# Attention with a double linear product: the weights' 64-bit words split on VectorE alone, with GpSimd left out

## The chip, the cores and the metric

The kernel runs on one core of one Trainium2 chip. The metric is the device time in microseconds, from three runs of the kernel before: 810.65 us median (810.63 to 811.8). One further execution was profiled, and the rows below come from it. PE is TensorE, PEld its loading of weights, DVE is VectorE, ACT is ScalarE, POOL is GpSimd, SP the engine that issues most loads.

## What is computed

Attention with a window and sinks (4 batches, 8 heads, 768 positions, 64 per head), then for all 3072 tokens a product of two linear projections, projected back. The text calls the second part the MoE, as the kernel does. The weights come as 64-bit floats, which the kernel reads as pairs of 32-bit words.

```python
scores = scale * np.matmul(q, k.transpose(0, 1, 3, 2))
keep = is_sink | in_window                 # pos < 4, or 0 <= rel < 128
a = softmax(where(keep, scores, -1e9))
x = (a @ v) as rows of 512                 # 3072 x 512
a = x @ w_a                                # 512 x 1536
b = x @ w_b
out = (a * b @ w_out)                      # 1536 x 512
```

## The kernel before

The tokens are taken in eight chunks of 2 to 4 tiles of 128 rows (CHUNKS). For each chunk the attention makes xf (four tiles of 128 features), `split_x` cuts it into a high half xh that TensorE reads in one pass (L667, ScalarE) and the rest xl (L668, VectorE), and `moe` runs 12 steps j over 128 of the 1536 inner features each: 12 matmuls for a, 12 for b (L686: high by high, high by low, low by high), their product g (L705 ScalarE, L711 VectorE), its halves gh (L714 ScalarE) and gl (L716), and one step later 3 matmuls per tile into the output (`project`, L695).

The attention of the first chunk runs alone: per unit (a head and a tile of rows) scores (L548, TensorE), the masked minimum (L555, VectorE), the exponential (L557, ScalarE), the normalisation (L559, L560, L562, VectorE), a transposition (L585) and the product with v (L602). Small copies for the sinks (L569) run on GpSimd. The attention of chunk c + 1 is woven into the MoE of chunk c, a few units per step, by `between`. The second chunk's attention has the same lines, with the normalisation on ScalarE (L564). From the third chunk on the attention is another form, in which GpSimd cuts q, k and v into halves (L345, L348).

There are 36 weight tiles of 128 x 512: a, b and o for each j, in this order. Each is loaded on SP's queue (L290) as 1024 32-bit words, low and high word in turns, and goes through stages that `weights_to` calls, one new tile per call:

- `weight_bits`: VectorE shifts the high word (L301) and joins sign and top bit to it (L303); ScalarE scales the low word (L302); GpSimd adds both (L305);
- three calls later `weight_high` (D1): ScalarE's cast to the high half (L312), into the tile that held the raw words;
- one call after that `weight_low` (D2): the low half (L317), a subtraction, on GpSimd for every third tile (all of b), else on VectorE.

The first seven calls lie in the first attention (from its step 18 on, every third step), the others in the first MoE, one in front of a's matmuls, one in front of b's and one in front of the projection of each j. Loads run up to 9 tiles ahead of the stage. gl (L716) runs on GpSimd for j below 10 and on VectorE for the last two.

Instructions given to `pin` (`keep_in_program_order`) keep the order of the program among themselves on their engine. All others, matmuls among them, are put where the framework's planner reckons that their operands are ready. L303, L305, L555, gl and the products g are such.

Of the kernel before, what the change touches and what calls it, by code (L numbers as in the profile page):

```python
# [7 lines left out]
F32 = mybir.dt.float32  # L8
# [5 lines left out]
ALU = mybir.AluOpType  # L14
# [3 lines left out]
B, H, S, D = 4, 8, 768, 64  # L18
DM, FF = 512, 1536
P = 128  # L20
# [3 lines left out]
NJ = FF // P  # L24
# [6 lines left out]
NEG = 8.0e9  # L31
BIG = 3.0e38
NIO = 6
POOL_LOW = (1, 3)
STEP0, STEPS = 18, 3
AHEAD, LOADS = 3, 9
D1, D2 = 3, 4
WARM = 8
H_MIN = 1.375 * 2.0 ** -12
H_SUM = 65536.0  # L40
# [1 line left out]
I_TOP2 = -1073741824  # L42
# [176 lines left out]
class Fast:  # L219
# [70 lines left out]
        self.nc.sync.dma_start(raw, self.src(kind)[j].bitcast(I32))  # L290
        self.raw[kind, j] = raw

    def low_engine(self, kind, j):
        return self.nc.gpsimd if (3 * j + "abo".index(kind)) % POOL_LOW[1] == POOL_LOW[0] else self.nc.vector

    def weight_bits(self, kind, j):
        nc, pin = self.nc, self.tc.keep_in_program_order
        rv = self.raw[kind, j].rearrange("p (n c) -> p n c", c=2)
        lo, hi = rv[:, :, 0], rv[:, :, 1]
        f = self.io([P, DM], I32, f"wf_{kind}{j}")  # L300
        pin(nc.vector.tensor_scalar(f, hi, 3, 0x3FFFFFF8, op0=ALU.logical_shift_left, op1=ALU.bitwise_and))  # L301
        pin(nc.scalar.activation(lo, lo.bitcast(U32), AF.Copy, scale=2.0 ** -29))  # L302
        nc.vector.scalar_tensor_tensor(out=f, in0=hi, scalar=I_TOP2, in1=f,  # L303
                                       op0=ALU.bitwise_and, op1=ALU.bitwise_or)
        nc.gpsimd.tensor_tensor(f, f, lo, op=ALU.add)  # L305
        del self.raw[kind, j]
        self.wf[kind, j] = f.bitcast(F32)

    def weight_high(self, kind, j):
# [3 lines left out]

    def weight_low(self, kind, j):
        wh, wl = self.wt[kind, j]
        e = self.low_engine(kind, j)
        i = e.tensor_tensor(wl, self.wf.pop((kind, j)), wh.bitcast(F32), op=ALU.subtract)  # L317
        if e is self.nc.vector:
            self.tc.keep_in_program_order(i)

    def check_weight(self, kind, j):

# [346 lines left out]
            xs.append((xh, xl))  # L669
        return xs  # L670

    def moe(self, row, nt, xf, between, weights_ahead, last):
        nc = self.nc
        n = nt * P
        tag = f"{row}"
        xs = self.split_x(xf, nt, tag)
        outs = [self.ps.tile([P, DM], F32, tag=("o0", "o1", "o2", "av")[i], name=f"o{tag}_{i}") for i in range(nt)]

        def half(kind, j):
            wh, wl = self.wt[kind, j]  # L680
            ps = self.ps.tile([P, 4 * P], F32, tag=kind, name=f"{kind}{tag}_{j}")
            for kk in range(NK):
                ksl = slice(kk * P, (kk + 1) * P)
                xh, xl = xs[kk]
                for i, (w, x) in enumerate(((wh, xh), (wh, xl), (wl, xh))):
                    nc.tensor.matmul(ps[:, :n], lhsT=w[:, ksl], rhs=x[:, :n],  # L686
                                     start=kk == 0 and i == 0, stop=kk == NK - 1 and i == 2)
            return ps

        def project(j, gh, gl):  # L690
            wh, wl = self.wt["o", j]
            for i in range(nt):
                sl = slice(i * P, (i + 1) * P)
                for k, (g, w) in enumerate(((gh, wh), (gh, wl), (gl, wh))):
                    nc.tensor.matmul(outs[i], lhsT=g[:, sl], rhs=w,  # L695
                                     start=j == 0 and k == 0, stop=j == NJ - 1 and k == 2)

        prev = None
        for j in range(NJ):
            if last and j == 2:  # L700
                self.ok = self.verdict(self.ps.tile([1, P], F32, tag="s", name="gp"))
            weights_ahead(3 * j)
            pa = half("a", j)
            g = self.mo.tile([P, max(n, 3 * P)], F32, tag="g", name=f"g{tag}_{j}", bufs=1)
            nc.scalar.copy(g[:, :n], pa[:, :n])  # L705
            between(3 * j)
            if last and j == NJ - 1:
                self.tc.mark_branch_hint_location("general", hint="LikelyTaken", engines=mybir.ALL_ENGINES)
            weights_ahead(3 * j + 1)
            pb = half("b", j)  # L710
            nc.vector.tensor_tensor(g[:, :n], pb[:, :n], g[:, :n], op=ALU.mult)  # L711
            gh = self.mo.tile([P, max(n, 3 * P)], F32R, tag="gh", name=f"gh{tag}_{j}")
            gl = self.mo.tile([P, max(n, 3 * P)], F32R, tag="gl", name=f"gl{tag}_{j}")
            nc.scalar.copy(gh[:, :n], g[:, :n])  # L714
            e = nc.vector if j >= NJ - 2 else nc.gpsimd
            e.tensor_tensor(gl[:, :n], g[:, :n], gh[:, :n].bitcast(F32), op=ALU.subtract)  # L716
            between(3 * j + 1)
            weights_ahead(3 * j + 2)
            if prev is not None:
                project(*prev)  # L720
            between(3 * j + 2)
            prev = (j, gh, gl)
        project(*prev)
        for i in range(nt):
            r = row + i * P
            o = self.mo.tile([P, DM], F32, tag=("gh", "gl")[i % 2], name=f"os{tag}_{i}")
            (nc.vector.tensor_copy if last and i == 1 else nc.scalar.copy)(o, outs[i])
            (nc.sync if last else nc.scalar).dma_start(self.out[r:r + P, :], o)
# [4 lines left out]
    def run(self, scalars, verdict):  # L733
        chunks = CHUNKS
        order = [(k, j) for j in range(NJ) for k in "abo"]
        done, loaded = [0], [0]

        def weights_to(n, ahead):
            while loaded[0] < min(n + ahead, len(order)):
                self.load_weight(*order[loaded[0]])  # L740
                loaded[0] += 1
            while done[0] < min(n + D2, len(order) + D2):
                k = done[0]
                for d, stage in ((D2, self.weight_low), (D1, self.weight_high), (0, self.weight_bits)):
                    if 0 <= k - d < len(order):
                        stage(*order[k - d])
                done[0] += 1

        b, t0, nt = chunks[0]

        pairs = [self.wp.tile([P, 2, nt * P], F32, tag=f"w_{k}{NJ - 1}", name=f"xf0_{k}") for k in "bo"]
        xf = [x[:, i, :] for x in pairs for i in range(2)]
        first = self.attention(b, t0, nt, xf, exact=True, alone=True)
        next(first)
        val = scalars()
        self.masks(val)
        self.verdict = lambda gp: verdict(val, gp)
        for k, _ in enumerate(first, 1):
            if k >= STEP0 and (k - STEP0) % STEPS == 0:
                weights_to(done[0] + 1 - D2, 4 + D2)  # L760
        for c, (b, t0, nt) in enumerate(chunks):
            gen = None
            if c + 1 < len(chunks):
                nb, nt0, nnt = chunks[c + 1]
                nxf = self.new_xf(c + 1)
                gen = self.attention(nb, nt0, nnt, nxf, exact=c == 0)
                steps = H * nnt + (6 if c else 5)
            taken = [0]

            def between(s):  # L770
                if gen is None:
                    return
                want = min(steps, -(-steps * (s + 1) // (3 * NJ - 3)))
                while taken[0] < want:
                    next(gen, None)
                    taken[0] += 1

            def ahead(s):
                j = s // 3
                weights_to(max(s + AHEAD, done[0] + 1 - D2), LOADS)  # L780
                if s % 3:
                    return
                k = (c - 2) * 8 + j - 2
                if c >= 2 and 2 <= j < 10 and k < len(order):
                    self.check_weight(*order[k])
                elif self.unchecked:
                    self.check_weight(None, 0)

            self.moe(b * S + t0 * P, nt, xf, between, ahead, c + 1 == len(chunks))
            if gen is not None:  # L790
                for _ in gen:
                    pass
                xf = nxf
        return val, self.ok
# [73 lines left out]
```

## Time and profile before

| | |
|---|---|
| median of three runs | 810.65 us |
| the profiled execution | 809.97 us |
| its span, first to last instruction | 808.1 us |
| TensorE busy | 787.8 us (97%) |
| VectorE, ScalarE, GpSimd busy | 433.8, 477.1, 381.0 us |
| additions L305 on GpSimd | 36, from 30 to 168 us |
| subtractions L317 | 12 on GpSimd, 24 on VectorE |
| gl L716 of the first MoE | 10 on GpSimd, 2 on VectorE |
| attention alone, first MoE | 0 to about 57.6 us, 57.6 to 188.5 us |

A matmul's end is modelled in such a profile, so a busy TensorE is not TensorE at its peak. A wait names the instruction that released the waiting one last. [...]

### The profile page before, as it was taken

Reading aid. Unit: us, or ns where it says so; the run is one execution under the profiler, and the core shown is the slowest. Engines: PE = TensorE matmul, PEld = TensorE weight load, DVE = VectorE, ACT = ScalarE, POOL = GpSimd, SP = SyncE. Lnnn points to the kernel's source line nnn. Section 1 sums busy time; section 2 is a strip of 40 time slices with the busy share of each in tenths; the row PEclk is TensorE's granted clock in tenths of the full one; section 3 lists DMA queues with packets and bytes.
Section 4 is the critical chain, followed back from the end, with each engine's and each line's share of the span. In section 5 each row is a group of like instructions: output and inputs, shape, how many; then the busy total and the mean of one; then the engine's idle time right before and its main releaser. Section 6 shows DMA issues by size and latency. Waiting matters only on the chain.

```text
span 808.1 us, 13597 instructions
## 1 busy us (share of the span) xinstructions
PE 787.8 (97%) x4457; PEld 697.4 (86%) x4457; DVE 433.8 (54%) x1427; ACT 477.1 (59%) x1384; POOL 381.0 (47%) x483
## 2 busy tenths in 40 slices
PE   8997999999999999999999999999999999999997
PEld 5655777778989999999999999999999999999996
DVE  6889877834663555445654455535554456430101
ACT  5775665636774766567774677647674678631111
POOL 1248665673772564626653466515646266301110
PEclk9999999999999999999999999999999999999999
DMA  8866430031221133413323133231334132001001
GB/s 311 299 219 256 172 103 21 11 95 63 67 67 63 46 108 115 119 59 103 102 89 102 65 107 105 93 105 48 108 115 124 54 105 61 1 2 39 1 1 41
DMA packets 44778, 76.11 MB, mean 94 GB/s; under 512 B 4640, under 2 KB 24224, under 8 KB 44704
## 3 DMA queue, kind: packets, MB, share of 16 engines
q1 hardware_dynamic: 41648, 69.70, 26.9%
q10 hardware_dynamic: 3024, 5.51, 1.8%
q8 instruction: 36, 0.59, 0.3%
q14 instruction: 38, 0.31, 0.1%
q0 software_dynamic: 32, 0.00, 0.0%
HBM read 68.90 MB, written 6.29 MB: 93 GB/s over the span
## 4 chain that ended last, share of the span: by engine, by line
PE 87%; DVE 8%; ACT 2%; issue 1%; POOL 0%; DVEq 0%; ACTq 0%; POOLq 0%
PE o L695 23%; PE a L686 23%; PE b L686 23%; PE t L451 4%; PE s L419 4%; PE av L467 3%; PE s L548 2%; PE av L602 1%; PE t L585 1%; PE t L602 1%; DVE wf_a L303 1%; DVE wf_a L301 1%; DVE p L562 1%; DVE g L711 1%; PE sk L492 1%
## 5 line engine op out<-in xcount | busy, mean ns | idle before, releaser
L686 PE MATMUL a<-xh,w_a 128*128 128x384 f32 (+2 forms) x768 | 218.9, 345 | 0.0
L686 PE MATMUL b<-xh,w_b 128*128 128x384 f32 (+2 forms) x768 | 215.2, 343 | 0.0
L695 PE MATMUL o<-w_o,gh 128*128 128x512 f32 x576 | 186.8, 404 | 0.0
L716 POOL TENSOR_TENSOR gl<-g,gh 128x384 fp32r<-128x384 f32 (+2 forms) x80 | 83.2, 1040 | 197.9 <-ACT gh L714 195.0
L686 PEld LDWEIGHTS a<-xh,w_a 128*128 128x128 f32 x768 | 138.7, 188 | 6.5 <-issue 1.5
L686 PEld LDWEIGHTS b<-xh,w_b 128*128 128x128 f32 x768 | 138.8, 188 | 4.5 <-issue 0.8
L711 DVE TENSOR_TENSOR g<-b,g 128x384 f32<-128x384 f32 (+2 forms) x96 | 53.4, 556 | 150.6 <-PE b L686 142.8
L686 PE MATMUL a<-xl,w_a 128*128 128x384 f32 (+2 forms) x384 | 129.2, 337 | 0.9 <-DVE xl L668 0.9
L686 PE MATMUL b<-xl,w_b 128*128 128x384 f32 (+2 forms) x384 | 129.0, 336 | 0.0
L695 PEld LDWEIGHTS o<-w_o,gh 128*128 128x128 f32 x576 | 104.0, 188 | 19.5 <-issue 1.0
L695 PE MATMUL o<-w_o,gl 128*128 128x512 f32 x288 | 113.7, 396 | 0.6 <-POOL gl L716 0.6
L714 ACT CAST gh<-g 128x384 fp32r<-128x384 f32 (+2 forms) x96 | 49.4, 514 | 79.7 <-DVE g L711 77.7
L705 ACT COPY g<-a 128x384 f32<-128x384 f32 (+2 forms) x96 | 45.1, 470 | 79.5 <-PE a L686 69.9
L430 ACT ACTIVATE p<-p,st 128x128 f32<-128x128 f32 (+1 forms) x144 | 71.4, 496 | 26.3 <-DVE st L429 25.4
L426 ACT ACTIVATE p<-p,st 128x128 f32<-128x128 f32 (+1 forms) x144 | 71.6, 497 | 8.4 <-DVE st L424 8.3
L686 PEld LDWEIGHTS a<-xl,w_a 128*128 128x128 f32 x384 | 72.4, 189 | 3.5 <-DVE xl L668 1.3
L686 PEld LDWEIGHTS b<-xl,w_b 128*128 128x128 f32 x384 | 72.4, 188 | 2.0 <-issue 0.3
L454 ACT CAST pt<-t 128x128 fp32r<-128x128 f32 (+1 forms) x144 | 50.4, 350 | 39.1 <-PE t L451 37.3
L455 DVE TENSOR_TENSOR pt<-t,pt 128x128 fp32r<-128x128 f32 (+1 forms) x144 | 57.1, 397 | 20.9 <-ACT pt L454 19.4
L695 PEld LDWEIGHTS o<-w_o,gl 128*128 128x128 f32 x288 | 54.1, 188 | 14.2 <-POOL gl L716 1.0
L345 POOL TENSOR_SCALAR qh<-qr 128x384 fp32r<-128x384 f32 x48 | 24.6, 512 | 75.3 <-PE s L419 43.8
L424 DVE CUSTOM_DVE_ANT_0 p<-s,mg 128x264 f32<-128x264 f32 x96 | 41.1, 428 | 34.7 <-PE s L419 34.4
(141 smaller groups left out, 1334.7 us busy)
## 6 DMA issues: line engine op xcount, KB each, us to landing
qr<-in_qT_dram SPq DMA_DIRECT2D x48, 192.0 KB, 2.6
raw_a<-in_wa_dram SPq DMA_DIRECT2D x12, 512.0 KB, 6.4
raw_b<-in_wb_dram SPq DMA_DIRECT2D x12, 512.0 KB, 5.7
raw_o<-in_wo_dram SPq DMA_DIRECT2D x12, 512.0 KB, 6.2
chk_a<-in_wa_dram SPq DMA_DIRECT2D x24, 256.0 KB, 2.7
chk_b<-in_wb_dram SPq DMA_DIRECT2D x24, 256.0 KB, 2.7
chk_o<-in_wo_dram SPq DMA_DIRECT2D x24, 256.0 KB, 2.7
out_dram<-os ACTq DMA_DIRECT2D x21, 256.0 KB, 2.1
```

The source lines that it names most:

```text
L419: nc.tensor.matmul(ps[:, :w], lhsT=q[:, i * P:(i + 1) * P], rhs=ks[:, c0:c0 + w], start=m == 0, stop=m == 1)
L424: nc.vector.tensor_tensor_reduce(out=p[:, :w], in0=ps[:, :w], in1=m, scale=-0.125, scalar=BIG, op0=ALU.add, op1=ALU.min, accum_out=st[:, 0:1])
L426: nc.scalar.activation(p[:, :w], p[:, :w], AF.Exp, bias=st[:, 0:1], scale=-1.0, accum_out=st[:, 1:2])
L430: nc.scalar.mul(p[:, :w], p[:, :w], st[:, 3:4])
L454: nc.scalar.copy(hs, tp[:, :n, :])
L455: nc.vector.tensor_tensor(ls, tp[:, :n, :], hs.bitcast(F32), op=ALU.subtract)
L686: nc.tensor.matmul(ps[:, :n], lhsT=w[:, ksl], rhs=x[:, :n], start=kk == 0 and i == 0, stop=kk == NK - 1 and i == 2)
L695: nc.tensor.matmul(outs[i], lhsT=g[:, sl], rhs=w, start=j == 0 and k == 0, stop=j == NJ - 1 and k == 2)
L705: nc.scalar.copy(g[:, :n], pa[:, :n])
L711: nc.vector.tensor_tensor(g[:, :n], pb[:, :n], g[:, :n], op=ALU.mult)
L714: nc.scalar.copy(gh[:, :n], g[:, :n])
L716: e.tensor_tensor(gl[:, :n], g[:, :n], gh[:, :n].bitcast(F32), op=ALU.subtract)
```

## The change

The addition L305 moves from `weight_bits` into a stage of its own, `weight_sum`, one call later, and from GpSimd to VectorE, pinned. L303 is pinned too. `weight_high` comes two calls after the bits instead of three, `weight_low` three instead of four. Every low half is taken on VectorE. `moe` learns by `weights_split` whether the weights are split already: in the first chunk they aren't, and gl is on VectorE for all twelve j; in the other chunks it stays where it was. Because D2 is one less, the count of loads issued in the first MoE is one ahead of before.

```diff
--- before.py
+++ after.py
@@ -31,10 +31,9 @@
 NEG = 8.0e9
 BIG = 3.0e38
 NIO = 6
-POOL_LOW = (1, 3)
 STEP0, STEPS = 18, 3
 AHEAD, LOADS = 3, 9
-D1, D2 = 3, 4
+D0, D1, D2 = 1, 2, 3
 WARM = 8
 H_MIN = 1.375 * 2.0 ** -12
 H_SUM = 65536.0
@@ -290,9 +289,6 @@
         self.nc.sync.dma_start(raw, self.src(kind)[j].bitcast(I32))
         self.raw[kind, j] = raw
 
-    def low_engine(self, kind, j):
-        return self.nc.gpsimd if (3 * j + "abo".index(kind)) % POOL_LOW[1] == POOL_LOW[0] else self.nc.vector
-
     def weight_bits(self, kind, j):
         nc, pin = self.nc, self.tc.keep_in_program_order
         rv = self.raw[kind, j].rearrange("p (n c) -> p n c", c=2)
@@ -300,10 +296,15 @@
         f = self.io([P, DM], I32, f"wf_{kind}{j}")
         pin(nc.vector.tensor_scalar(f, hi, 3, 0x3FFFFFF8, op0=ALU.logical_shift_left, op1=ALU.bitwise_and))
         pin(nc.scalar.activation(lo, lo.bitcast(U32), AF.Copy, scale=2.0 ** -29))
-        nc.vector.scalar_tensor_tensor(out=f, in0=hi, scalar=I_TOP2, in1=f,
-                                       op0=ALU.bitwise_and, op1=ALU.bitwise_or)
-        nc.gpsimd.tensor_tensor(f, f, lo, op=ALU.add)
-        del self.raw[kind, j]
+        pin(nc.vector.scalar_tensor_tensor(out=f, in0=hi, scalar=I_TOP2, in1=f,
+                                           op0=ALU.bitwise_and, op1=ALU.bitwise_or))
+        self.wf[kind, j] = f
+
+    def weight_sum(self, kind, j):
+
+        f = self.wf[kind, j]
+        lo = self.raw.pop((kind, j)).rearrange("p (n c) -> p n c", c=2)[:, :, 0]
+        self.tc.keep_in_program_order(self.nc.vector.tensor_tensor(f, f, lo, op=ALU.add))
         self.wf[kind, j] = f.bitcast(F32)
 
     def weight_high(self, kind, j):
@@ -313,10 +314,8 @@
 
     def weight_low(self, kind, j):
         wh, wl = self.wt[kind, j]
-        e = self.low_engine(kind, j)
-        i = e.tensor_tensor(wl, self.wf.pop((kind, j)), wh.bitcast(F32), op=ALU.subtract)
-        if e is self.nc.vector:
-            self.tc.keep_in_program_order(i)
+        self.tc.keep_in_program_order(
+            self.nc.vector.tensor_tensor(wl, self.wf.pop((kind, j)), wh.bitcast(F32), op=ALU.subtract))
 
     def check_weight(self, kind, j):
 
@@ -669,7 +668,7 @@
             xs.append((xh, xl))
         return xs
 
-    def moe(self, row, nt, xf, between, weights_ahead, last):
+    def moe(self, row, nt, xf, between, weights_ahead, last, weights_split):
         nc = self.nc
         n = nt * P
         tag = f"{row}"
@@ -712,7 +711,7 @@
             gh = self.mo.tile([P, max(n, 3 * P)], F32R, tag="gh", name=f"gh{tag}_{j}")
             gl = self.mo.tile([P, max(n, 3 * P)], F32R, tag="gl", name=f"gl{tag}_{j}")
             nc.scalar.copy(gh[:, :n], g[:, :n])
-            e = nc.vector if j >= NJ - 2 else nc.gpsimd
+            e = nc.gpsimd if weights_split and j < NJ - 2 else nc.vector
             e.tensor_tensor(gl[:, :n], g[:, :n], gh[:, :n].bitcast(F32), op=ALU.subtract)
             between(3 * j + 1)
             weights_ahead(3 * j + 2)
@@ -741,7 +740,7 @@
                 loaded[0] += 1
             while done[0] < min(n + D2, len(order) + D2):
                 k = done[0]
-                for d, stage in ((D2, self.weight_low), (D1, self.weight_high), (0, self.weight_bits)):
+                for d, stage in ((D2, self.weight_low), (D1, self.weight_high), (D0, self.weight_sum), (0, self.weight_bits)):
                     if 0 <= k - d < len(order):
                         stage(*order[k - d])
                 done[0] += 1
@@ -786,7 +785,7 @@
                 elif self.unchecked:
                     self.check_weight(None, 0)
 
-            self.moe(b * S + t0 * P, nt, xf, between, ahead, c + 1 == len(chunks))
+            self.moe(b * S + t0 * P, nt, xf, between, ahead, c + 1 == len(chunks), c > 0)
             if gen is not None:
                 for _ in gen:
                     pass
```

## Rows read from the trace of the kernel before

**Rows 1.** Stretches: us, busy PE, PEld, DVE, ACT, POOL (instructions), clock, DMA share, GB/s

```profile
20.00:57.60 37.60, 35.70 (x194) 22.65 (x193) 31.56 (x131) 29.38 (x87) 11.89 (x20) 1.00 0.73 254
57.60:88.00 30.40, 23.64 (x98) 17.56 (x98) 28.60 (x40) 18.33 (x40) 24.87 (x20) 0.94 0.65 245
...
100.00:146.00 46.00, 44.68 (x210) 33.71 (x209) 35.71 (x71) 29.06 (x65) 28.22 (x28) 1.00 0.19 60
...
188.50:802.00 613.50, 610.92 (x3625) 569.96 (x3624) 290.09 (x1057) 361.89 (x1100) 277.43 (x368) 1.00 0.24 73
```

**Rows 2.** Who TensorE waited for: us in all, times, longest us

```profile
PE s L548 <- DVE st L555: 5.9, 3, 5.3
...
PE a L686 <- DVE xl L668: 0.9, 1, 0.9
...
PE o L695 <- POOL gl L716: 0.6, 1, 0.6
```

**Rows 3.** Timeline, 75.5 to 82 us: start us, us, engine, line, operation, [idle before]

```profile
75.67 1.46 POOL L716 TENSOR_TENSOR gl<-g,gh 128x512 fp32r<-128x512 f32 x1
...
76.04 1.65 DVE L303 SCALAR_TENSOR_TENSOR wf_a<-raw_a,wf_a 128x512 int32<-128x512 int32 x1
...
78.21 1.48 DVE L301 TENSOR_SCALAR wf_b<-raw_b 128x512 int32<-128x512 int32 x1
...
79.73 1.65 DVE L303 SCALAR_TENSOR_TENSOR wf_b<-raw_b,wf_b 128x512 int32<-128x512 int32 x1
81.30 0.42 DVE L555 CUSTOM_DVE_ANT_0 p<-s,mg 128x264 f32<-128x264 f32 x1
...
81.78 0.81 PE L548 MATMUL s<-kx,qx 128*128 128x264 f32 x1 [5.25 <-DVE st L555]
```

**Rows 4.** The stretch behind the stall, columns as in rows 1

```profile
81.40:84.90 3.50, 3.12 (x11) 2.11 (x11) 2.61 (x9) 2.65 (x6) 2.07 (x3) 0.51 0.76 308
```

**Rows 5.** Single lines: engine, operation, count: shortest/median/longest ns, first to last start us

```profile
L301 DVE TENSOR_SCALAR wf_b<-raw_b x12: 396/415/1539, 32.3 to 157.6; 128x512 int32<-128x512 int32 x12
...
L303 DVE SCALAR_TENSOR_TENSOR wf_b<-raw_b,wf_b x12: 677/691/1677, 33.0 to 158.1; 128x512 int32<-128x512 int32 x12
...
L305 POOL TENSOR_TENSOR wf_b<-wf_b,raw_b x12: 1286/1306/1767, 33.8 to 161.2; 128x512 int32<-128x512 int32 x12
...
L317 DVE TENSOR_TENSOR w_a<-wf_a,w_a x12: 669/682/1783, 47.8 to 169.3; 128x512 fp32r<-128x512 f32 x12
...
L562 DVE TENSOR_SCALAR p<-p,st x21: 273/350/1237, 20.2 to 50.1; 128x264 f32<-128x264 f32 x16, 128x128 f32<-128x128 f32 x5
...
L668 DVE TENSOR_TENSOR xl<-xf_o,xh x2: 681/1252/1824, 46.3 to 57.5; 128x512 fp32r<-128x512 f32 x2
```

**Rows 6.** Busy time of L301 alone: 57.6 to 88, and 20 to 188.5

```profile
57.60:88.00 30.40, 8.08 (x9) 0.94 0.65 245
...
sum 168.50, DVE 29.66; mean DVE 9.89
```

**Rows 7.** The same of L303 alone

```profile
57.60:88.00 30.40, 9.03 (x9) 0.94 0.65 245
...
sum 168.50, DVE 33.18; mean DVE 11.06
```

**Rows 8.** The same of L317 alone, GpSimd's part second

```profile
57.60:88.00 30.40, 7.37 (x6) 5.18 (x3) 0.94 0.65 245
...
sum 168.50, DVE 24.05 POOL 17.95; mean DVE 8.02 POOL 5.98
```

**Rows 9.** The same of L562 alone, 20 to 57.6 us

```profile
20.00:57.60 37.60, 10.76 (x21) 1.00 0.73 254
```

**Rows 10.** Timeline: first matmul of j = 3; fifth a's low half, its first use

```profile
88.02 0.40 PE L686 MATMUL a<-xh,w_a 128*128 128x512 f32 x1
...
88.39 0.68 DVE L317 TENSOR_TENSOR w_a<-wf_a,w_a 128x512 fp32r<-128x512 f32 x1
...
98.56 0.50 PE L686 MATMUL a<-xh,w_a 128*128 128x512 f32 x1
```

## The prediction

> **What bounds the kernel now.** I read the busy time by stretches first [rows 1], because a mean over 808 us hides where TensorE stands still. From 188.5 us on, TensorE is busy 610.92 of 613.5 us; VectorE and GpSimd there cost nothing, and the change alters nothing in that part. The weights are split before that. 20 to 57.6 us is the second half of the first attention, which runs alone; at 57.6 us the first MoE gets its last inputs, and by 88 us it runs evenly. In 57.6 to 88 TensorE is busy 23.64 of 30.4 us at a mean granted clock of 0.94, while VectorE is busy 28.60. In 100 to 146 TensorE misses 1.3 us. So whatever the change can give, it must give almost wholly in that one stretch of 30 us.
>
> The table of who waited for whom names the 6.8 us lost there [rows 2]: one wait of 5.3 us of the scores (L548) for the softmax's first VectorE step (L555), 0.9 us for the low half of the attention output (L668), 0.6 us for gl on GpSimd (L716). In order of time [rows 3] the long one is plain: VectorE has L555 behind four weight instructions, and three of these take 1.48 to 1.65 us. GpSimd runs weight and gate subtractions beside them. [...]
>
> Why are they long? Each line has two durations [rows 5]: L301 takes 0.40 to 0.42 us or 1.5, L303 0.68 or 1.68, L317 0.67 or 1.78, the same form each time. The long durations lie beside a GpSimd instruction of this size [rows 3], the quiet ones beside none. GpSimd's own add also stretches, 1.29 to 1.77. I read it as one engine standing still while the other holds what both need.
>
> **The change, part by part.** *The queue.* Per weight VectorE gets one addition (L305) and, for every b, the subtraction (L317) that GpSimd had; per j of the first MoE the gate's subtraction, ten times. No row shows the integer addition on VectorE. Its nearest row is L303: the same 512 columns, int32, one input at a stride of two words, two inputs from SBUF: 0.68 to 0.69 us quiet. The ends are L301's 0.41 and L305's 1.29 on GpSimd [rows 5]; I take 0.69. Nothing here excludes that it is a little cheaper. Added: 36 x 0.69 + 12 x 0.675 + 10 x 0.675 = 39.7 us.
>
> [...]
>
> *What it takes away.* With no large GpSimd instruction beside them, the weight instructions fall to their quiet durations. From the sums by line over 20 to 188.5 us [rows 6 to 9]: L301 29.66 - 36 x 0.415 = 14.7; L303 33.18 - 36 x 0.69 = 8.3; L317 24.05 - 24 x 0.675 = 7.9. L562 of the attention took up to 1.24 instead of 0.35 (0.28 for the short form), 10.76 - 16 x 0.35 - 5 x 0.28 = 3.8; one xl took 1.82 instead of 0.68, 1.1 [rows 5]. Together 35.8 us. **So VectorE gets about 4 us more work over the whole stage, not less.** The gain can't come from a lighter VectorE; it must come from where and when.
>
> *57.6 to 88 us.* By the same sums for this stretch [rows 6 to 8], removed: 8.08 - 9 x 0.415 = 4.3; 9.03 - 9 x 0.69 = 2.8; 7.37 - 6 x 0.675 = 3.3; xl 1.1; sum 11.5. Added: 9 sums, 3 lows of b, 3 gl: 6.2 + 2.0 + 2.0 = 10.2. VectorE would need 28.6 - 1.3 = 27.3 us for the same work, TensorE 23.64 - 1.5 = 22.1. If TensorE gets through in 22 us, VectorE is some 5 us of weights behind where it is today. There is room: the low half of the fifth a ends at 89.07 and is first used at 98.56 [rows 10], 9.5 us ahead. For the first three j the lead is smaller, and there the shorter pipeline helps: the low half comes three steps after the bits instead of four, which takes one step's bits and sum (about 1.8 us) out of what stands in front of the low halves of j = 1 to 3.
>
> *The stall.* Matmuls, L303, L555 and gl are not pinned; the planner places them where it reckons their operands to be ready. L555 behind 5.3 us of weight words that belong to later steps is not an order that anyone plans; I take it that the planner reckons with the quiet durations, and that the order would fit if they held. With no contention they hold. Then L555 finds at most one weight instruction in front of it: 0.69 + 0.42 = 1.1 us of the 5.25 stay. Gain 4.1, at least 0 and at most 5.25. The half clock came right behind the stall; I count 1.5 with it. The xl: 1.1 us shorter, of which TensorE waited 0.9. The gl of j = 0 runs right behind gh on VectorE instead of behind two additions in GpSimd's queue: 0.6.
>
> *20 to 57.6 us.* VectorE is busy 31.56 of 37.6 [rows 1]. It gets six sums and two lows (one that the shorter pipeline brings forward, one of b), 6 x 0.69 + 2 x 0.675 = 5.5, and gives back 3.8 of L562: +1.7 us on an engine with 6 us free [rows 1, 9]. Cost: at least -1 us (the softmax's chain gets shorter where L562 was slow), at most 5.5 if all of it lies in front of softmax steps and none of L562 was on the path; I take 0.5, as the engine has room. What waits behind a weight word here is L555 and so the next scores on TensorE.
>
> *100 to 188.5 us.* TensorE misses 1.3 us up to 146 [rows 1]; I leave that. GpSimd loses what it does for the weights and keeps the small copies (L569), and later gets to the next attention's halves sooner; nobody waits for these. Loads are issued one weight earlier in the MoE, at cost nothing: SP's queue leads by several weights there. ScalarE does the same instructions, its L312 one step earlier.
>
> **Sum**: -0.9 - 0.6 - 4.1 - 1.5 + 0.5 = -6.6 us. The profiled execution took 809.97 us (span 808.1), so 803.4; the median of the runs is 810.65, so **804.0**.
>
> **The rivals.** (1) *The stall stays.* If the planner keeps the order, L555 stands behind the same four instructions, quiet 2.47 us, plus two sums, a low of b and a gl, 2.73: 5.2 us, what it is today. Half clock too. Only xl, gl and the 0.5 remain: 809.6. For it: VectorE's work is no less. Against: an order made with true durations should not leave L555 there. (2) *VectorE is the bound of 57.6 to 88*: 27.3 us instead of 30.4, 3.1 gained, 807.5. For it: the engine is busy 94% there. Against: it need not do all that work by then [rows 10]. (3) *Slower*: the weight words stand in front of the softmax in the attention alone. Each step is 0.41 + 0.69 + 0.69 + 0.675 = 2.5 us of VectorE where it was 1.1 plus a third GpSimd work; if 5.5 us come onto the path there, L562 gives nothing back because its long durations were off the path, and the stall stays as in (1), it is 810.65 + 5.5 - 1.5 = 814.7. It decides once the added VectorE time in 20 to 57.6 that lies on the path passes what 57.6 to 88 gives. Against: 6 us free there. (4) *Everything goes*, all idle time of TensorE from 57.6 to 188 and the half clock, 6.8 + 1.3 + 1.5 = 9.6, and 1.9 of 20 to 57.6: 799.1. (5) *The addition runs slow on VectorE*, at its upper end of 1.29 us [rows 5], 0.60 more each: 9 x 0.60 = 5.4 on the 27.3 us of 57.6 to 88 make 32.7 where the stretch takes 30.4 now, +2.3; of 6 x 0.60 = 3.6 more in the attention alone I count 0.5: 813.5. Against: the quiet rows of L303, which read the words in the same steps.
>
> [...]
>
> **How the numbers follow.** Forecast (800.5 to 806.5) 0.60; everything goes 0.05; VectorE bound 0.12; stall stays 0.10; slower 0.10; slow addition 0.03. About 0.2% is what a measurement of this kernel can tell from no change, 809.0 to 812.3: faster 0.77, same 0.11, slower 0.12. The range leaves out the slow ends and half of the unlikely best: 799.5 to 811.0.
>
> **What would show it.** L301, L303 and L317 with one duration each, below 0.42, 0.70 and 0.70; the sum at 0.69 on VectorE; VectorE's busy time from 20 to 188 about as now; no wait of several us of L548 for L555; j = 3 of the first MoE, which began at 88.02 [rows 10], at 80 to 82 us; the full clock throughout; the rest shifted as a whole. I'd be wrong if L548 still waits for L555, if the attention alone ends later than 57.6 us by more than 1, or if TensorE waits for w_a.

## The result, and the profile after

| | before | after |
|---|---|---|
| median | 810.64 us | 801.92 us (800.92 to 803.06) |
| the profiled execution, its span | 809.97, 808.1 us | 800.92, 799.0 us |
| ratio | | 0.9888 (95%: 0.9873 to 0.9903) |

8.7 us were gained where 6.6 were forecast; 801.92 lies inside the range of 800.5 to 806.5. Line numbers of the changed kernel differ a little: L301 is L297, L303 is L299, L305 (now on VectorE) L307, L317 is L318, L548 is L547, L555 is L554, L562 is L561, L668 is L667, L716 is L715.

The stretches after, columns as in [rows 1]:

```profile
20.00:57.60 37.60, 36.01 (x194) 22.67 (x193) 31.66 (x134) 28.83 (x85) 5.76 (x13) 1.00 0.75 266
57.60:88.00 30.40, 29.15 (x133) 23.06 (x132) 27.89 (x66) 21.80 (x47) 4.58 (x4) 1.00 0.84 304
...
100.00:146.00 46.00, 46.00 (x220) 35.32 (x219) 40.76 (x99) 31.32 (x73) 3.01 (x8) 1.00 0.05 14
...
179.40:793.00 613.60, 610.94 (x3623) 569.70 (x3621) 290.28 (x1057) 361.44 (x1100) 277.42 (x368) 1.00 0.24 73
```

In 57.6 to 88 TensorE has 29.15 us of work where it had 23.64, at the full clock; in 100 to 146 nothing is missing; GpSimd went from 24.87 us to 4.58 in the first of these. VectorE is as busy as before, 27.89 us against 28.60, and has more to do from 100 to 146 (40.76 against 35.71). The last stretch has the length of before: the MoE after the first and all that follows moved as a whole, 9.1 us earlier.

The weight lines and the softmax's L561, shortest/median/longest as in [rows 5]:

```profile
L297 DVE TENSOR_SCALAR wf_a<-raw_a x12: 408/420/424, 28.5 to 146.5; 128x512 int32<-128x512 int32 x12
...
L299 DVE SCALAR_TENSOR_TENSOR wf_a<-raw_a,wf_a x12: 670/686/693, 29.2 to 147.0; 128x512 int32<-128x512 int32 x12
...
L307 DVE CUSTOM_DVE_ANT_0 wf_a<-raw_a,wf_a x12: 660/684/689, 32.0 to 148.2; 128x1024 uint16<-128x1024 uint16 x12
...
L307 DVE CUSTOM_DVE_ANT_0 wf_o<-raw_o,wf_o x12: 672/684/1517, 41.6 to 157.7; 128x1024 uint16<-128x1024 uint16 x12
...
L318 DVE TENSOR_TENSOR w_b<-wf_b,w_b x12: 660/683/686, 48.0 to 159.9; 128x512 fp32r<-128x512 f32 x12
...
L561 DVE TENSOR_SCALAR p<-p,st x21: 278/351/361, 20.2 to 50.8; 128x264 f32<-128x264 f32 x16, 128x128 f32<-128x128 f32 x5
```

Up to 148 us each has one duration now, and the sum, an instruction of its own form over 1024 halves of words, takes 0.684 us. Seven of the 144 weight instructions still take 0.75 to 1.52 us (one is the 1517 in the row for o). All seven start between 148.8 and 160.6 us, and at 148.52 GpSimd begins to cut q, k and v for the next attention (L344, L347). The softmax's step no longer stands behind a row of long instructions, as it did in [rows 3]; the timeline around it, start us, us, engine, line:

```profile
72.37 0.42 DVE L297 TENSOR_SCALAR wf_o<-raw_o 128x512 int32<-128x512 int32 x1
72.71 0.43 DVE L554 CUSTOM_DVE_ANT_0 p<-s,mg 128x264 f32<-128x264 f32 x1
...
73.06 0.69 DVE L299 SCALAR_TENSOR_TENSOR wf_o<-raw_o,wf_o 128x512 int32<-128x512 int32 x1
74.35 0.43 DVE L554 CUSTOM_DVE_ANT_0 p<-s,mg 128x264 f32<-128x264 f32 x1 [0.60 <-PE s L547]
```

And TensorE's three longest waits from 20 to 180 us, against [rows 2]:

```profile
PE a L685 <- ACT xh L666: 1.0, 1, 1.0
PE av L601 <- ACT ptx L585: 0.4, 1, 0.4
PE s L547 <- DVE st L554: 0.3, 1, 0.3
```

The wait of 5.3 us is gone. What is left is a wait of 1.0 us for the high half xh on ScalarE, in the place of the 0.9 for xl.

### The profile page after: what moved, and what is told of

It is laid out like the page before. It is cut to its first block, busy times and chain, and to the rows that moved or that the text cites. A ratio compares the mean times of both kernels' runs of the same rounds, so it can differ in the third digit from the quotient of the medians.

```text
span 799.0 us, 13573 instructions
## 1 busy us (share of the span) xinstructions
PE 785.5 (98%) x4457; PEld 697.2 (87%) x4457; DVE 433.3 (54%) x1485; ACT 475.8 (60%) x1384; POOL 307.1 (38%) x425
## 4 chain that ended last, share of the span: by engine, by line
PE 92%; DVE 4%; ACT 3%; DMA 1%; issue 1%; POOL 0%; DVEq 0%; POOLq 0%; ACTq 0%
PE a L685 25%; PE o L694 24%; PE b L685 24%; PE t L450 4%; PE s L418 4%; PE av L466 3%; PE s L547 2%; PE av L601 2%; PE t L584 1%; PE t L601 1%; PE sk L491 1%; ACT p L425 1%; DVE g L710 0%; ACT xf L471 0%; DVE xf L472 0%
## 5 line engine op out<-in xcount | busy, mean ns | idle before, releaser
L694 PE MATMUL o<-w_o,gh 128*128 128x512 f32 x576 | 186.9, 404 | 0.0
L715 POOL TENSOR_TENSOR gl<-g,gh 128x384 fp32r<-128x384 f32 (+1 forms) x70 | 68.2, 974 | 201.1 <-ACT gh L713 198.3
L694 PEld LDWEIGHTS o<-w_o,gh 128*128 128x128 f32 x576 | 104.0, 188 | 19.3 <-issue 0.8
L694 PE MATMUL o<-w_o,gl 128*128 128x512 f32 x288 | 113.6, 395 | 0.0
L694 PEld LDWEIGHTS o<-w_o,gl 128*128 128x128 f32 x288 | 54.1, 188 | 13.1 <-DVE gl L715 0.8
L568 POOL COPY sc<-p 128x8 f32<-128x8 f32 x32 | 15.7, 490 | 128.7 <-ACT p L563 86.6
```

Of the source, the lines that this page charges most:

```text
L694: nc.tensor.matmul(outs[i], lhsT=g[:, sl], rhs=w, start=j == 0 and k == 0, stop=j == NJ - 1 and k == 2)
```

## Experiments

Two theories. **One**: GpSimd and VectorE hold each other up, and the gain is that no large GpSimd instruction runs beside VectorE. **Two**: the pins, the shorter pipeline and another order of instructions give the gain. Medians are us; ratios are to the kernel before on the same chip. The experiments ran in three sets on three chips, where the kernel before took 810.4, 810.98 and 811.13 us; distances to the changed kernel are to its 801.92 where nothing else is said, so one of less than about 1 us says little. In the last set (the kernel before without GpSimd's reads, and the depths a second time) the changed kernel ran too and gave 801.55 us. Edits are shown by the lines that matter. Where an edit adds a line, the line numbers behind it move by one or two.

### The changed kernel with GpSimd work that nobody uses

```diff
         self.wf[kind, j] = f
+        nc.gpsimd.tensor_tensor(hi, lo, lo, op=ALU.add)
```

> The changed kernel with one idle GpSimd addition per weight (128x512, reads the scaled low words, writes the high words that nobody needs any more): nobody uses its result, and the order of instructions on TensorE, VectorE and ScalarE is the same as in the changed kernel. Theory 1 (the two engines hold each other up; the gain is the absence of large GpSimd instructions beside VectorE): the weight lines on VectorE have two durations again, VectorE gets 15 to 30 us more from 20 to 180 us, TensorE waits several us for VectorE before 90 us, 807 to 816 us. Theory 2 (the gain is the planner's new order, the pins and the shorter pipeline): below 804 us.

812.59 us, ratio 1.0023 (1.0008 to 1.0038): 10.7 us above the changed kernel, although no instruction waits for the result other than the later write of that tile. The order on TensorE, VectorE and ScalarE is untouched: from 10 to 170 us the two traces show it the same, instruction by instruction. From 20 to 180 us VectorE is busy 145.05 us where it was 129.69, 15.4 more, and TensorE waits for L555 four times, 4.2 us in all. The sum of b on VectorE, as in [rows 5]:

```profile
L308 DVE CUSTOM_DVE_ANT_0 wf_b<-raw_b,wf_b x12: 666/1335/1531, 38.0 to 165.1; 128x1024 uint16<-128x1024 uint16 x12
```

One meeting in the timeline, columns as in [rows 3]:

```profile
77.21 1.42 POOL L302 TENSOR_TENSOR raw_b<-raw_b 128x512 int32<-128x512 int32 x1
77.66 1.53 DVE L308 CUSTOM_DVE_ANT_0 wf_b<-raw_b,wf_b 128x1024 uint16<-128x1024 uint16 x1
79.44 0.42 DVE L555 CUSTOM_DVE_ANT_0 p<-s,mg 128x264 f32<-128x264 f32 x1
...
79.92 0.71 PE L548 MATMUL s<-kx,qx 128*128 128x264 f32 x2 [2.01 <-DVE st L555]
```

The sum starts beside GpSimd's addition, ends 0.56 us after that has ended, at 79.19, and so looks like 0.6 us of work behind a wait; L555 and with it TensorE's scores stand behind it. Of the 36 sums 16 start while an idle addition runs, and 13 of these take 1.15 to 1.53 us. The low halves and gl get longer too: 791 to 858 ns on the mean of a tile's twelve where the changed kernel has 678 to 758, and 907 where it has 691. L297 does not (at most 0.43 us), since the idle addition comes behind it, so this part of the expectation was missed. Doubled:

```diff
         self.wf[kind, j] = f
+        for _ in range(2):
+            nc.gpsimd.tensor_tensor(hi, lo, lo, op=ALU.add)
```

> The same with two idle additions per weight. Theory 1: longer again, by at least as much as the first idle addition cost, 812 to 830 us, since VectorE is nearly full. Theory 2: as with one, below 804 us.

838.36 us, ratio 1.0323 (1.0282 to 1.0364): 36.4 us above the changed kernel, more than was expected at the most. VectorE has hardly any room left: it is busy 57.98 of 60 us from 120 to 180. But this run is no longer contention alone, since others now wait for the idle additions themselves: ScalarE's casts 16.7 us in all, and once TensorE (us, times, longest):

```profile
PE t L614 <- POOL raw_o L303: 2.6, 1, 2.6
```

The single addition shows the cause more cleanly. Theory two would have left both below 804; as the whole explanation it falls.

### The same place, but GpSimd reads nothing

```diff
         self.wf[kind, j] = f
+        for _ in range(2):
+            nc.gpsimd.memset(hi, 0)
```

> The changed kernel with two idle GpSimd fills per weight (128x512, they read nothing and write the high words that nobody needs any more), in the place of the idle addition of the run beside; same order on TensorE, VectorE and ScalarE. If any GpSimd instruction of this size holds VectorE up: as with the idle addition, 808 us or more. If what the two engines share is above all a way to read: the lines with two inputs from SBUF (the sum, L299, the low halves) keep their short durations, only the one-input L297 and L561 get longer, 801 to 805 us.

802.31 us, ratio 0.9888 (0.9865 to 0.9910), as the changed kernel. The profiled executions of this run and of the one with a single idle addition both have a lower clock in the attention alone (0.91 on the mean from 20 to 57.6 us), so that their spans can be compared: 802.5 and 811.8 us. The sum of b, as in [rows 5]:

```profile
L309 DVE CUSTOM_DVE_ANT_0 wf_b<-raw_b,wf_b x12: 674/686/689, 38.3 to 154.7; 128x1024 uint16<-128x1024 uint16 x12
```

The fills behind b's bits: shapes, count, busy us, mean ns, idle before:

```profile
L303 POOL MEMSET raw_b<- 128x512 int32 x24 | 13.7, 571 | 8.2 <-DVE wf_b L299 7.4
```

Two fills of 0.57 us per weight are about as much GpSimd time as one addition, at the same place, and VectorE's sum never gets longer than 0.69 for b. 17 of the 36 sums start while a fill runs, and none of these takes more than 0.69. So in these two runs it is not GpSimd's being busy that costs, but its reading: the sum of b, with two inputs from SBUF, took up to 1.53 us beside the additions and at most 0.69 beside the fills. That the one-input lines get longer, as the expectation had it, the trace hardly shows. The softmax's one-input step (L561 in the changed kernel) reaches 0.60 us where 0.36 was the most; L297, also with one input, takes 0.45 us at most, but the fills that it meets end less than 0.2 us after its start.

### The kernel before without GpSimd's reads

```diff
-        nc.gpsimd.tensor_tensor(f, f, lo, op=ALU.add)
+        for _ in range(2):
+            nc.gpsimd.memset(f, 0)
```

and in the same way for the low halves of b and for the ten gl of the first MoE.

> The kernel before, with each large GpSimd instruction of the weights and of the first MoE's gate (36 sums, 12 low halves of b, 10 gl) replaced by two fills of the same tile, which read nothing; the sums and these low halves are left out of the result. The order of instructions on TensorE, VectorE and ScalarE is that of the kernel before, and so is VectorE's own work. If the stall of the kernel before is contention and not its order: the wait of 5.3 us and the half clock behind it are gone, 799 to 803 us. If it is the order: the wait stays, 808 us or more.

798.05 us, ratio 0.9831 (0.9807 to 0.9855). With the sums left out the weights are zeros; a matmul of 128x512 takes 0.39 to 0.40 us as before. Its stretch of 57.6 to 88 us, columns as in [rows 1]:

```profile
57.60:88.00 30.40, 30.40 (x139) 24.21 (x138) 24.59 (x57) 23.96 (x52) 21.09 (x42) 1.00 0.79 284
```

Its L301 for o and its L303 for b, as in [rows 5]:

```profile
L301 DVE TENSOR_SCALAR wf_o<-raw_o x12: 408/460/1327, 37.1 to 147.1; 128x512 int32<-128x512 int32 x12
...
L303 DVE SCALAR_TENSOR_TENSOR wf_b<-raw_b,wf_b x12: 673/693/697, 33.0 to 146.5; 128x512 int32<-128x512 int32 x12
```

TensorE is busy 30.40 of 30.40 us at the full clock, in the very order of the kernel before: from 10 to 170 us the two traces have the same instructions in the same order on TensorE, VectorE and ScalarE. So the stall of [rows 3] was no fault of that order: it fits VectorE's short durations, and contention made them false. L303, with two inputs, keeps one duration beside the fills (0.67 to 0.70 us in all 36), while L301, with one, still takes 0.7 to 0.9 us six times and 1.33 once, each time beside fills. So this one-input line does get longer beside fills, in seven of its 36 executions. The distance to the changed kernel in the same set is 3.5 us. VectorE's additional work and another order of instructions both lie in it; what each costs was not measured.

### One part back on GpSimd at a time

All three (sums, low halves of b, gl), with the pins and depths of the change (the comments name the place of each line):

```diff
+        self.nc.gpsimd.tensor_tensor(f, f, lo, op=ALU.add)            # weight_sum
+        e = self.nc.gpsimd if kind == "b" else self.nc.vector         # weight_low
+        e = nc.gpsimd if j < NJ - 2 else nc.vector                    # gl
```

> The changed kernel's stages, pins and depths (1, 2, 3), but the sums, the low halves of b and ten gl of the first MoE on GpSimd as before. Theory 1: the contention is back, 808 to 812 us, as before the change. Theory 2 (pins and the shorter pipeline give the gain): 801 to 804 us.

815.4 us, ratio 1.0053 (1.0038 to 1.0069): 13.5 us above the changed kernel and even 5 above the kernel before. As long as GpSimd has its work, the pins and the shorter pipeline bring nothing. Why it is above the kernel before I didn't settle. Between the two profiled spans, 813.7 and 808.1 us, 2.6 of the 5.6 us lie in the attention alone, whose last step on VectorE starts at 58.81 us where it started at 56.25. Its trace also shows one long wait of TensorE at another place (us, times, longest):

```profile
PE t L603 <- ACT ptx L587: 5.4, 1, 5.4
```

It is of the same kind as before: the copy ptx stands behind a step of the softmax on ScalarE, and that behind VectorE's reciprocal (here L561), in front of which VectorE has weight lines of 1.50 and 1.80 us again:

```profile
79.94 1.50 DVE L297 TENSOR_SCALAR wf_b<-raw_b 128x512 int32<-128x512 int32 x1
...
81.47 1.80 DVE L299 SCALAR_TENSOR_TENSOR wf_b<-raw_b,wf_b 128x512 int32<-128x512 int32 x1
...
83.63 0.51 ACT L565 ACTIVATE p<-p,st 128x264 f32<-128x264 f32 x1 [2.45 <-DVE st L561]
```

A stretch at the half clock (0.51) follows, columns as in [rows 1]:

```profile
84.30:91.20 6.90, 6.25 (x19) 5.00 (x20) 5.95 (x12) 5.40 (x13) 4.81 (x6) 0.51 0.00 1
```

Only the sums:

```diff
-        self.tc.keep_in_program_order(self.nc.vector.tensor_tensor(f, f, lo, op=ALU.add))
+        self.nc.gpsimd.tensor_tensor(f, f, lo, op=ALU.add)
```

> The changed kernel with only the 36 sums back on GpSimd, low halves and gl on VectorE. Theory 1: 50 us of the 83 us of GpSimd work are back beside VectorE: 804 to 809 us. Theory 2 (the chain over GpSimd was what cost, gl and low halves of b above all): 801 to 803 us.

808.85 us, ratio 0.9977 (0.9959 to 0.9996): 6.9 above the changed kernel, within what theory one expected.

Only the low halves of b:

```diff
+        e = self.nc.gpsimd if kind == "b" else self.nc.vector
```

> The changed kernel with the 12 low halves of b back on GpSimd. By contention: 18 of the 83 us of GpSimd work are back, 802.5 to 805 us. If only the sums did harm: 801 to 802.5 us.

806.3 us, ratio 0.9946 (0.9929 to 0.9962): 4.4 above, more than expected.

Only gl of the first MoE:

```diff
-            e = nc.gpsimd if weights_split and j < NJ - 2 else nc.vector
+            e = nc.gpsimd if j < NJ - 2 else nc.vector
```

> The changed kernel with ten gl of the first MoE back on GpSimd. By contention: 15 of the 83 us are back, 802.5 to 805 us, and VectorE has 6.8 us less of its own. If only the sums did harm: 800.5 to 802.5 us.

804.24 us, ratio 0.9924 (0.9906 to 0.9941): 2.3 above. Together 6.9 + 4.4 + 2.3 = 13.6 us, and all three at once cost 13.5; that they agree so closely is chance, since each interval is 1.2 to 1.5 us wide to either side. None of the three is idle in the change. How much of each is contention, and how much the longer way over GpSimd, these runs don't separate; the idle additions above show contention alone.

### The depths

```diff
-D0, D1, D2 = 1, 2, 3
+D0, D1, D2 = 1, 3, 4
```

> The changed kernel with the depths 1, 3, 4 instead of 1, 2, 3: high and low half come one call later, as before the change. If the shorter pipeline is a part of the gain: TensorE waits for w_a at j = 1 or 2, 803 to 805 us. If the absence of contention is all: 801 to 803 us.

800.52 us, ratio 0.9875 (0.9858 to 0.9891), just below what either theory expected. TensorE doesn't wait for w_a. Once more beside the changed kernel, in five rounds:

> The changed kernel with the depths 1, 3, 4, a second time beside the changed kernel itself. If the depth gives something: 0.5 to 1.5 us below it. If not: the same within 0.2%.

> The changed kernel itself on the same chip, for the comparison with the depths 1, 3, 4: 801 to 803 us.

800.54 us, ratio 0.9871 (0.9851 to 0.9891), and the changed kernel 801.55 us, 0.9881 (0.9860 to 0.9903). The difference of 1.0 us has the same sign twice, but the intervals overlap almost wholly. The longer pipeline costs nothing; that it gains is not shown.

## Why the prediction held, and where not

The direction, the place and the mechanism were right: contention between GpSimd and VectorE in 57.6 to 88 us, seen in the two durations of each line, made the one long wait, and the wait went with it. The sizes of the terms were not all right, and part of the closeness of the total is errors that cancel. By the steps of the working, in us of the profiled executions:

- *Long beside GpSimd, quiet beside none*: half right. Of the 36 L303 of the kernel before, nine start while a GpSimd addition or subtraction runs, and take 1.21 to 1.84 us; GpSimd's instruction takes 1.30 to 1.51 there. But six start first, have such an instruction begin beside them, and take 0.68 or 0.69; there it is GpSimd's instruction that gets longer, 1.67 us in the rows below and 1.33 to 1.44 in the other five, where the shortest L305 takes 1.28 and the shortest L317 on GpSimd 1.31. So here the one that started later lost the most.
- *The sum at 0.69*: measured 0.684. It runs as a form over halves of words; L299, which reads every second word, takes 0.686, as forecast from [rows 5].
- *VectorE gets no lighter*: the forecast was 4 us more over the whole stage. From 20 us to the end of the first MoE its busy time is 130.25 us before and 129.69 after (rows below), 0.6 less, with 58 instructions more; in 20 to 88 us it went from 60.16 [rows 1] to 59.55. The point on which the forecast turned holds: the stage ends 9.4 us earlier with VectorE as busy as before, so the gain comes from when and not from how much.
- *The attention alone, +0.5*: its last step on VectorE (L626, now L625) starts at 56.83 us where it started at 56.25, +0.6, as forecast. But the last xl starts at 58.93 where it started at 57.52, +1.4. The rest comes from ScalarE: before, xh followed that step at once; now a copy for the next chunk's attention (ptx, L585) stands in front of xh and itself waits for a transposition on TensorE (rows below), so that xh starts 1.03 us after the end of that step. This place in the new order was not foreseen. By the start of the last xl, one of the signs named for being wrong, an attention that ends later by more than 1, came true.
- *xl, -0.9*: this failed as a term of its own. xl takes 0.69 instead of 1.82, but TensorE now waits 1.0 for the xh in front of it, which is late for the reason just given. What was late next should have been named.
- *gl, -0.6*: gone; no projection waits for gl any more.
- *The stall, 1.1 of 5.25 left*: nothing of it is left. From 58.9 to 80.6 us TensorE is busy 21.43 of 21.70 us.
- *The half clock, -1.5*: gone, 1.00 throughout up to the end of the last matmuls. No row of before shows the 1.5 us itself, only 3.12 us of matmuls at 0.51 [rows 4]. The two traces together show it: from two matmuls of scores (L548, now L547) over eight with v (L602, now L601) to the next projection (L695, now L694) it was 3.08 us at that clock (81.78 to 84.86 us) and is 1.55 at 1.00 in the changed kernel (75.90 to 77.45), 1.5 less.
- *100 to 188.5, counted at nothing*: mis-sized. From the start of j = 3 to the end of the first MoE it was 100.4 us and is 98.4, of which 1.3 were the missing work of [rows 1]: two waits of 0.66 us for a copy on ScalarE (L604). What held that copy up was not followed; the waits are gone.

L303 started first and GpSimd's addition after it, in the kernel before, columns as in [rows 3]:

```profile
72.16 0.68 DVE L303 SCALAR_TENSOR_TENSOR wf_o<-raw_o,wf_o 128x512 int32<-128x512 int32 x1
...
72.32 1.67 POOL L305 TENSOR_TENSOR wf_b<-wf_b,raw_b 128x512 int32<-128x512 int32 x1 [0.97 <-DVE wf_b L303]
```

The whole stage before and after, columns as in [rows 1]:

```profile
20.00:188.50 168.50, 158.51 (x749) 116.13 (x748) 130.25 (x293) 102.95 (x246) 100.52 (x100) 0.99 0.41 143
...
20.00:179.40 159.40, 156.56 (x751) 116.20 (x750) 129.69 (x351) 102.17 (x246) 26.71 (x42) 1.00 0.44 151
```

The last xh in the kernel before, then in the changed one, columns as in [rows 3]:

```profile
56.25 0.42 DVE L626 TENSOR_TENSOR xf_o<-sk,xf_o 128x256 f32<-128x256 f32 x1 [0.99 <-PE sk L624]
...
56.71 0.62 ACT L667 CAST xh<-xf_o 128x512 fp32r<-128x512 f32 x1
...
58.01 0.37 ACT L585 COPY ptx<-t 128x256 f32<-128x256 f32 x1 [1.59 <-PE t L584]
...
58.28 0.62 ACT L666 CAST xh<-xf_o 128x512 fp32r<-128x512 f32 x1
```

The first MoE from j = 3 on in the kernel before, columns as in [rows 1]:

```profile
88.00:188.40 100.40, 99.08 (x458) 75.82 (x457) 70.09 (x124) 55.14 (x121) 63.76 (x61) 1.00 0.23 70
```

The changed kernel from its last xl to j = 3, and from there to the end of the first MoE:

```profile
58.90:80.60 21.70, 21.43 (x97) 16.94 (x98) 20.68 (x46) 15.88 (x34) 2.73 (x3) 1.00 0.86 322
80.60:179.00 98.40, 98.40 (x458) 76.11 (x457) 76.75 (x171) 56.17 (x126) 18.22 (x27) 1.00 0.22 70
```

Its last xl and its first matmul of j = 3 in the timeline, columns as in [rows 3]:

```profile
58.93 0.69 DVE L667 TENSOR_TENSOR xl<-xf_o,xh 128x512 fp32r<-128x512 f32 x1 [0.73 <-ACT xh L666]
...
80.59 0.39 PE L685 MATMUL a<-xh,w_a 128*128 128x512 f32 x1
```

From the last xl to j = 3 it was 88.02 - 57.52 = 30.5 us and is 80.59 - 58.93 = 21.7. So +1.4 - 8.8 - 2.0 = -9.4, and behind the first MoE +0.3: -9.1, the difference of the spans. The forecast had +0.5 - 7.1 and nothing for the other two, -6.6: too little for the attention alone, and too little gain in both stretches of the MoE. j = 3 at 80.6 is inside the 80 to 82 that was named.

- *The shorter pipeline helps at j = 1 to 3*: not borne out. With the old depths the kernel is as fast.
- *The planner reckons with the quiet durations*: this was argued in the prediction. The order of before is now shown to run without the stall once GpSimd reads nothing, and the order on the other three engines came out the same with GpSimd's additions and with fills in their place. So the planned order does not answer to this contention; which durations the planner holds was not looked at.

Of the rivals, the one that everything goes (799.1) came nearest besides the forecast: of TensorE's idle time from the last xl to the end of the first MoE all but 0.3 us went, while the attention alone got longer instead of shorter. Rival 1's sum, 5.2 us in front of L555 before and after, counted the instructions in the old order; in the new order TensorE waits 0.3 us for that step. The longer attention of rival 3 is there in kind, at 0.6 us and not 5.5. Of rival 5, the addition that runs slow, nothing is seen.

## What to carry to other kernels

Where a line of VectorE has two durations for one form, look for what GpSimd reads at the time, and which of the two started first: here 0.42, 0.69 and 0.67 us became 1.5 to 1.8. Not every line does this: the product g (L711), one of whose two operands is in PSUM, took 677 to 692 ns in all twelve executions of the kernel before, although four of them start while an addition L305 runs. Work moved from GpSimd onto a VectorE that was over 90% busy still gained here, 8.7 us, since the engine gave back in waits what it took on in work: in 57.6 to 88 us it was busy 28.60 us with 40 instructions and is 27.89 with 66. A sum over the stretch from quiet durations told beforehand that VectorE would have room, not how much would be gained. GpSimd instructions that only write cost nothing measurable here (802.31 against 801.92 us) but weren't free in every place: the one-input L301 reached 1.33 us beside fills.

## What I hadn't expected of the hardware

The half clock also comes where no long wait is named. In the profiled execution of the kernel before with fills, the granted clock in the attention alone was 0.57 over 4 us, with TensorE busy 3.60 of them and its longest wait from 40 to 50 us 0.5 us:

```profile
42.00:46.00 4.00, 3.60 (x12) 2.11 (x12) 3.36 (x15) 3.64 (x13) 2.29 (x5) 0.57 0.73 249
```

The changed kernel's profiled execution has none there. Its four executions take 800.92 and 801.07 us at a mean clock of 0.999, 802.78 at 0.997 and 803.06 at 0.996; as an estimate, 0.003 of 801 us is 2.4 us, so the clock alone could account for the 2 us between them. Differences of this size between two kernels need several executions of each.
